# A two-layer attention and gated feed-forward network, forward and backward: transposes by DMA in place of TensorE, weights loaded in pieces, attention products paired, blocks of the feed-forward swapped

## The chip, the cores and the metric

One core of one Trainium2 chip. The time is device microseconds of one execution, the median of several runs. Times inside an execution come from one profiled execution, counted from the start of its span. The engines are TensorE (PE, with weight loads as PEld), VectorE (DVE), ScalarE (ACT), GpSimd (POOL) and SyncE (SP). Every DMA of this kernel is issued from SP's queue, in order: a DMA that has to wait holds up every DMA behind it.

## The reference

The network applies block A, block B, block A, block B to x of shape 2048 x 512, each with a layer normalisation before and a residual around it. The weights of both A blocks are the same, and those of both B blocks. The result is the output and the gradients of x and of all weights, by reverse differentiation from `grad_out`.

```python
def _A_ref(x, wqkv, wo):                      # linear attention, 32 heads of 16
    q, k, v = split_heads(x @ wqkv)
    phi = lambda t: jnp.where(t > 0, t + 1, jnp.exp(t)) + 1e-6
    pq, pk = phi(q), phi(k)
    kv = jnp.einsum("bhsd,bhse->bhde", pk, v)
    z = jnp.einsum("bhsd->bhd", pk)
    num = jnp.einsum("bhqd,bhde->bhqe", pq, kv)
    den = jnp.einsum("bhqd,bhd->bhq", pq, z)[..., None] + 1e-6
    return merge_heads(num / den) @ wo
def _B_ref(x, w_gate, w_up, w_down):          # F = 1376
    h = _sigmoid(x @ w_gate) * (x @ w_up)
    return h @ w_down
x = x + _A_ref(_layernorm(x), A_wqkv, A_wo)   # layer 0
x = x + _B_ref(_layernorm(x), B_w_gate, B_w_up, B_w_down)   # layer 1
x = x + _A_ref(_layernorm(x), A_wqkv, A_wo)   # layer 2
x = x + _B_ref(_layernorm(x), B_w_gate, B_w_up, B_w_down)   # layer 3
```

## The kernel before

The 2048 rows are 16 tiles (`NST`) of 128 rows; two tiles are a pair, four are a block (`NBLK` = 4, 512 rows). D = 512 is four chunks of 128, F = 1376 is eleven chunks (`NFC`), the last of 96.

The order of stages is: `kq_fwd` for layer 0 (keys and queries), `ab_fwd` for layers 0 and 1 together, `kq_fwd` for layer 2, `ab_fwd` for layers 2 and 3, then backward: `BBwd(3).run`, `ABwd(2).first` and `.second`, `BBwd(1).run`, `ABwd(0).first` and `.second`, with the products for the weights' gradients (`p2_gen`) filled in between and at the end.

The order on TensorE, ScalarE, VectorE and GpSimd is the order in which the code issues (`manual_schedule` over these four, `EM`). SP isn't among them. Its order is chosen by the planner of the framework from modelled times, when a DMA's operands are ready there; `issue_after(ins)` only makes a DMA follow another one. On the chip SP then works through that order and waits where something isn't ready yet.

**`ab_fwd`** (line 1050 and on; in the change and below, layer 1 or 3 names its feed-forward half `l`). It goes through the pairs `i` of tiles, `st = 2 * i`. In one pass it does six units of the feed-forward for pair `i`, the second product of the feed-forward (`down_mm`) for the pair before, and the attention for the pair after.

- `gu(st, 2, *CUNITS[u])`: gate and up products of unit `u`: two chunks of F, unit 5 a single one. On TensorE a unit of two is 16 matmuls of 256 columns into the banks `g` and `u` (line 1070). ACT writes the sigmoid into the tile `ssd_t` (line 1086, three buffers) and one minus it into `oms` (1087), DVE the product into `hhT` (1088), POOL the second half of `ssd_t` (1089), and SP stores `ssd_t` (1092). The next use of an `ssd_t` buffer waits for that store.
- `trans`: VectorE transposes `hhT` in blocks into `tr_stg` (1039, two buffers) and SP stores it (1042).
- `ln.apply`, `ln.stage_T`: the normalised rows `hstage`, turned on TensorE (line 568, eight transposes of 128 x 128) into bank `t`, copied by ACT into `hT`, which the next pair's `gu` reads.
- `pair_prod` (POOL), `pair_front1` and `pair_front2` (DVE; the latter ends with `pqnstage`, line 968, stored to DRAM by SP at line 971 for the backward pass) make the normalised queries of pair `i + 2`. `pair_front3` turns them: eight transposes on TensorE (line 982) and an ACT copy (983) into `pqnT2`. `attn_y` of each tile (four matmuls, line 995) then reads them in the next round, right behind the first unit for the first tile and behind the second unit for the second tile; DVE adds the result to x (1003) and takes the statistics of the next normalisation.
- In layer 3, `turn_weights` sends one job at a time of the list from `wT_dmas_b` (line 455 and on), at places between the units: turned loads of `w_down` into `wdT` and their stores, then loads of `wuT` and `wgT`, which `kq_fwd` of layer 2 has turned already, from DRAM. These are the weights of the backward pass.

**`BBwd.run`** (from line 1431) is the backward pass of a feed-forward. For each block of 512 rows and each chunk `u` of F, `D` multiplies `wdT` by the turned gradient `gT` (four matmuls of 512 columns, line 1385), two steps ahead (`LOOK`); ACT copies (1391), DVE and POOL multiply with the stored `ssd` (1392, 1393); `H` multiplies with `wuT` and `wgT` (eight matmuls, line 1417). At the end of a block the normalisation's gradient follows, spread over the next block's steps. `gT` of the next block is made in two halves by `make_gT`: eight transposes on TensorE each (line 1356) and an ACT copy (1357), at steps 5 and 6. In layer 3 (`first`) the gradient is the input `grad_out`, loaded by `load_g` (1337); block 0's is made within the last round of `ab_fwd`, and in block 2 the steps are 7 and 8, with one `D` put behind its `H` (`behind`). In layer 1 the gradient is in `k.xs` in float32; `cast_g` casts it on ACT at steps 1 to 4 into `gstage` (1343) and SP stores it to DRAM as `gbf` (1345), which a later stage reads.

## Time and profile before

| | |
|---|---|
| median of 3 runs | 1132.63 us (1131.1 to 1133.29) |
| profiled execution | 1131.85 us, its span 1130.1 us |
| mean granted TensorE clock | 0.997 |
| TensorE idle in the span, all causes | 35.7 us |
| `ab_fwd` of layer 1 | about 70 to 210 us |
| `ab_fwd` of layer 3 | about 275 to 414 us, transfer engines busy 62% |
| `BBwd` of layer 3 | about 407 to 530 us, transfer engines busy 86% from 414 on |
| `BBwd` of layer 1 | about 737 to 856 us, transfer engines busy 76% from 740 on |
| share of DMA queue q1 over the span | 79.0% |

How to read it: a row of a group gives line, engine, operation, tiles, shape and count, then the group's busy time in us, the mean of one instruction in ns, and the idle time just before such instructions with what ended it. Matmuls are pipelined, so the mean of one is longer than the distance from one to the next. In a timeline a row is start and duration in us, and in brackets the idle time before it and what it waited for. A row of SP with a large duration holds up SP's queue for that long.

### The profile page before, as it was taken

What the parts mean: (1) busy time and instruction counts of PE and PEld (TensorE: products, weight loads), DVE (VectorE), ACT (ScalarE), POOL (GpSimd) and SP (SyncE); (2) the same over time, 40 slices, a digit from 0 to 9 for tenths busy, and PEclk for the clock granted to TensorE, in tenths of its full rate; (3) what the DMA queues carried; (4) which work ended last, traced back from release to release, by engine and by line L of the source; (5) the groups of instructions that cost most, each with busy time, mean ns of one, the idle gap of its engine ahead of it and who ended that gap; (6) DMA issues with size and microseconds to landing.
All of it is one profiled execution on the core that took longest, in us unless ns stands there. A gap on an engine that the chain in (4) does not pass through costs nothing. (4 is left out here: it accounts for less than half of the span.)

```text
span 1130.1 us, 20199 instructions
## 1 busy us (share of the span) xinstructions
PE 1094.4 (97%) x7453; PEld 673.3 (60%) x7556; DVE 718.7 (64%) x1263; ACT 501.9 (44%) x924; POOL 468.1 (41%) x627
## 2 busy tenths in 40 slices
PE   7999999999999899999999999999999999999998
PEld 4467767546776654444665556544446756555577
DVE  7887887888678567776993640057778955642221
ACT  4676656557656533444552441145545523420001
POOL 3738776433766445776110440047772101420000
PEclk9999999999999999999999999999999999999999
DMA  7955657695666768978789967887768999958997
GB/s 218 319 169 160 199 177 222 198 263 177 173 217 187 235 201 265 303 232 278 214 235 265 280 192 253 296 283 225 224 214 223 268 276 253 258 194 272 274 253 166
DMA packets 342612, 263.02 MB, mean 233 GB/s; under 512 B 105648, under 2 KB 321136, under 8 KB 342512
## 3 DMA queue, kind: packets, MB, share of 16 engines
q1 hardware_dynamic: 342512, 261.72, 79.0%
q8 instruction: 59, 0.97, 0.4%
q14 instruction: 41, 0.34, 0.1%
HBM read 122.62 MB, written 119.47 MB: 214 GB/s over the span
## 5 line engine op out<-in xcount | busy, mean ns | idle before, releaser
L1694 PE MATMUL p_ps<-p_set,p_a 128*128 128x384 bf16 (+2 forms) x1792 | 264.6, 304 | 3.3 <-DMA p_set<-sv_hdd 1.5
L1694 PEld LDWEIGHTS <-p_a 128*128 128x128 bf16 x1792 | 168.7, 96 | 87.2 <-issue 3.4
L1393 POOL TENSOR_TENSOR dd<-dhb,ssd 128x512 bf16<-128x512 bf16 x84 | 96.7, 1156 | 106.1 <-ACT dhb L1391 103.9
L1392 DVE TENSOR_TENSOR dd<-dhh_ps,ssd 128x512 bf16<-128x512 f32 x85 | 57.2, 679 | 123.1 <-ACT dhb L1391 121.3
L1417 PE MATMUL dh_ps<-wuT,dd 128*128 128x512 bf16 (+1 forms) x340 | 129.0, 379 | 0.7
L1089 POOL TENSOR_TENSOR ssd_t<-hhT,oms 128x512 bf16<-128x512 bf16 (+1 forms) x92 | 99.7, 1092 | 71.8 <-DVE hhT L1088 50.4
L1417 PE MATMUL dh_ps<-wgT,dd 128*128 128x512 bf16 (+1 forms) x325 | 123.3, 380 | 0.0
L1417 PEld LDWEIGHTS <-dd 128*128 128x128 bf16 x680 | 66.3, 98 | 79.7
L1070 PE MATMUL g_ps<-hT,wg 128*128 128x256 bf16 (+1 forms) x792 | 93.6, 262 | 6.5 <-ACT oms L1087 5.4
L1709 DVE TENSOR_TENSOR dw_stg<-p_ps,dw_stg 128x384 bf16<-128x384 f32 (+2 forms) x76 | 32.0, 438 | 106.4 <-PE p_ps L1694 99.1
L1070 PE MATMUL u_ps<-hT,wu 128*128 128x256 bf16 (+1 forms) x792 | 93.5, 262 | 3.0 <-DVE hhT L1088 3.0
L1391 ACT CAST dhb<-dhh_ps 128x512 bf16<-128x512 f32 x84 | 48.7, 588 | 99.5 <-PE dhh_ps L1385 86.6
L1088 DVE TENSOR_TENSOR hhT<-u_ps,ssd_t 128x512 bf16<-128x512 f32 (+1 forms) x92 | 57.5, 629 | 51.5 <-ACT ssd_t L1086 49.2
L1086 ACT ACTIVATE ssd_t<-g_ps 128x512 bf16<-128x512 f32 (+1 forms) x92 | 51.7, 562 | 86.6 <-PE g_ps L1070 44.4
L1039 DVE STREAM_TRANSPOSE tr_stg<-dd 128x768 f32<-128x768 f32 (+1 forms) x62 | 86.6, 1437 | 1.1
L1070 PEld LDWEIGHTS <-wg 128*128 128x128 bf16 x792 | 70.1, 98 | 27.2 <-issue 8.0
L1385 PE MATMUL dhh_ps<-gT,wdT 128*128 128x512 bf16 x301 | 77.2, 379 | 1.6 <-DVE dd L1392 0.7
L1105 PE MATMUL y_ps<-wd,hhT 128*128 128x512 bf16 (+1 forms) x337 | 77.7, 380 | 0.8
L1070 PEld LDWEIGHTS <-wu 128*128 128x128 bf16 x792 | 70.9, 98 | 12.0 <-issue 4.6
L1711 ACT CAST dw_stg<-p_ps 128x384 bf16<-128x384 f32 (+2 forms) x76 | 28.0, 385 | 88.6 <-PE p_ps L1694 83.8
L1385 PEld LDWEIGHTS <-wdT 128*128 128x128 bf16 x352 | 33.8, 97 | 41.7 <-issue 3.8
L516 POOL TENSOR_TENSOR rstd_all<-rstd_all,neghalf 128x1 f32<-128x1 f32 x64 | 37.9, 592 | 47.7 <-DVE rstd_all L515 43.1
(256 smaller groups left out, 1919.3 us busy)
## 6 DMA issues: line engine op xcount, KB each, us to landing
sv_hdd<-tr_stg SPq DMA_DIRECT2D x72, 384.0 KB, 4.6
p_set<-sv_hdd SPq DMA_DIRECT2D x18, 1536.0 KB, 7.4
sv_ssd<-ssd_t SPq DMA_DIRECT2D x74, 256.0 KB, 2.6
ssd<-sv_ssd SPq DMA_DIRECT2D x23, 768.0 KB, 5.2
h_ld<-sv_h SPq DMA_DIRECT2D x30, 256.0 KB, 4.1
sv_hdl<-tr_stg SPq DMA_DIRECT2D x24, 256.0 KB, 4.8
p_a<-sv_h SPq DMA_DIRECT2D x12, 512.0 KB, 6.5
p_set<-sv_hdl SPq DMA_DIRECT2D x24, 256.0 KB, 4.9
```

The costliest lines, as they stand in the source:

```text
L1039: nc.vector.transpose(t[:, :, 0:n * P].bitcast(F32).rearrange("p q (a j) -> p q a j", a=2 * n), src.rearrange("p c x -> p (c x)").bitcast( ...
L1070: nc.tensor.matmul(ps[:, ci * n:(ci + 1) * n], lhsT=w_sb[:, kc, (c0 + ci) * P:(c0 + ci + 1) * P], rhs=hT[:, kc, (st % 2) * P:(st % 2) * P ...
L1086: nc.scalar.activation(ssd[:, :, 0, :], gv, ACT.Sigmoid)
L1088: nc.vector.tensor_tensor(hh, uv, ssd[:, :, 0, :], ALU.mult)
L1089: nc.gpsimd.tensor_tensor(ssd[:, :, 1, :], hh, oms, ALU.mult)
L1105: nc.tensor.matmul(y_ps[:], lhsT=h[0:r, fc, off:off + P], rhs=k.wd[0:r, fc, :], start=(fc == 0), stop=(fc == NFC - 1))
L1385: nc.tensor.matmul(ps[:], lhsT=k.wdT[:, jc, u * P:(u + 1) * P], rhs=self.gT[B][:, jc, :], start=(jc == 0), stop=(jc == NDC - 1))
L1391: nc.scalar.copy(dhb[:], ps[:])
L1392: nc.vector.tensor_tensor(self.dd[ng][:, 0, c, :], ps[:], self.ssd[ng][:, c, 0, :], ALU.mult)
L1393: nc.gpsimd.tensor_tensor(self.dd[ng][:, 1, c, :], dhb[:], self.ssd[ng][:, c, 1, :], ALU.mult)
L1417: nc.tensor.matmul(self.acc[j][:], lhsT=dd[0:r, a, c, j * P:(j + 1) * P], rhs=w[0:r, u, :], start=(u == 0 and a == 0), stop=(u == NFC - 1 ...
L1694: nc.tensor.matmul(ps[:, 0:w], lhsT=lhs[:, s, ic * P:(ic + 1) * P], rhs=rhs, start=(s == 0), stop=(s == NST - 1))
```

## The change

- `wT_dmas_b`: `wuT` and `wgT` are loaded in five pieces of two chunks each (256 KB) in place of a piece of six chunks and one of four. In layer 3 `turn_weights` is called at up to four places of a round in place of one or two.
- `pair_front3`: the turned queries are loaded from DRAM, where `pair_front2` has stored them, by a transposing DMA on SP, in place of eight transposes and a copy. The early pair of each pass is still turned on TensorE.
- `attn_y` of both tiles of a pair stand together behind the first unit.
- The units 4 and 5 of the feed-forward are swapped around `stage_T`, except in the last round; `pair_front3` stands ahead of both.
- In layer 1's pass `ssd_t` has five buffers, in a pool of its own, and `tr_stg` four.
- `BBwd`: `turn_g` loads `gT` by two transposing DMAs, in layer 3 from the input for all blocks, in layer 1 from the stored `gbf` at step 6 for the blocks 1 to 3. Block 0 of layer 1 is still turned on TensorE. The special order in block 2 of layer 3 goes, but for the late load of its `gstage`.

```diff
@@ wT_dmas_b
-        for c, e in ((0, 6), (6, NFC - 1)):
+        for c in range(0, NFC - 1, 2):
+            e = c + 2
             jobs.append(lambda nm=nm, t=t, c=c, e=e: nc.sync.dma_start(out=t[:, c:e, :],
                                                                        in_=view(k.wT[nm + "T"][c * P:e * P, :])))
@@ attn_fronts
-    def pair_front3(i):
+    def pair_front3(i, dma=True):
...
+        if dma:
+            turned = pool.tile([P, NDC, 2 * P], BF16, name="pqnT2", bufs=2)[:]
+            nc.sync.dma_start_transpose(out=turned, in_=sva["pqn"][batch_rows(i, 2), :])
+            pqnT = turned.rearrange("p c (n t) -> p n c t", n=2)
+        else:
...
@@ ab_fwd
+        more = ctx.enter_context(tc.tile_pool(name=f"bf_more{l}", bufs=5, reuse_waits="tile")) if l == 1 else None
...
-                ssd_f = work.tile([P, 2 * BT], BF16, name="ssd_t", bufs=3)
+                ssd_f = (more or work).tile([P, 2 * BT], BF16, name="ssd_t", bufs=5 if more else 3)
...
-            block_transposes(k, work, sv, 0, B, g, hhT[B][:, c0:c0 + nch, :], bufs=2)
+            block_transposes(k, work, sv, 0, B, g, hhT[B][:, c0:c0 + nch, :], bufs=4 if l == 1 else 2)
...
-        A.pair_front3(2)
+        A.pair_front3(2, False)
...
             gu(st, 2, *CUNITS[0])
+            if l == 3 and i > 1:
+                turn_weights()
             A.attn_y(st + 2, "t")
+            A.attn_y(st + 3, "t")
             A.pair_front1(i + 2)
             after(st - 3)
             gu(st, 2, *CUNITS[1])
-            A.attn_y(st + 3, "t")
             A.pair_front2(i + 2)
...
             if l == 3 or i % 2 == 0:
                 turn_weights()
-                if l == 3 and i > 3:
-                    turn_weights()
...
             gu(st, 2, *CUNITS[3])
+            if l == 3:
+                turn_weights()
             down_mm(st - 1, "t")
...
-                if bwd is not None:
-                    bwd.make_gT(0, 0)
-            gu(st, 2, *CUNITS[4])
+            A.pair_front3(i + 2)
+            gu(st, 2, *CUNITS[5 if not last else 4])
             ln.stage_T([st + 2, st + 3], bank="t")
-            A.pair_front3(i + 2)
             after(st - 2)
-            if last and bwd is not None:
-                bwd.make_gT(0, 1)
-            gu(st, 2, *CUNITS[5])
+            gu(st, 2, *CUNITS[4 if not last else 5])
+            if l == 3:
+                turn_weights()
@@ BBwd.load_g
         if self.first:
+            self.turn_g(B)
             nc.sync.dma_start(out=t[:], in_=dram_batch(k.g_in, B))
+    def turn_g(self, B):
+        if B not in self.gT:
+            self.gT[B] = self.alloc(False, "work", [P, NDC, BT], "gT", 2)
+        for half in range(2):
+            self.k.nc.sync.dma_start_transpose(out=self.gT[B][:, :, half * 2 * P:(half + 1) * 2 * P],
+                                               in_=self.sv["gbf"][batch_rows(2 * B + half, 2), :])
@@ BBwd.run
-                    behind = self.first and B == 2 and u == 9
...
-                    if not close and not behind:
+                    if not close:
                         self.D(n + self.LOOK)
                     self.H(B, u)
-                    if behind:
-                        self.D(n + self.LOOK)
...
-                        if u in ((7, 8) if late else (5, 6)):
-                            self.make_gT(B + 1, 0 if u in (5, 7) else 1)
+                        if u == 6 and not self.first:
+                            self.turn_g(B + 1)
```

More of the change, by code (lines that the diff above doesn't have):

```diff
@@ L977, in pair_front3 @@
         pqn = F_[2 * i]["pqn"]
-        pqnT = pool.tile([P, 2, NDC, P], BF16, name="pqnT2", bufs=2)
-        ps = ps_tile(k, "ln", [P, 2, NDC, P], BF16, "ln_tp")
-        for j in range(2):
-            for c in range(NDC):
-                nc.tensor.transpose(ps[:, j, c, :], pqn[:, j, c * P:(c + 1) * P], k.ident[:])
-        nc.scalar.copy(pqnT[:], ps[:])
+        if dma:
[3 more added lines that the diff above has]
+        else:
+            pqnT = pool.tile([P, 2, NDC, P], BF16, name="pqnT2", bufs=2)[:]
+            ps = ps_tile(k, "ln", [P, 2, NDC, P], BF16, "ln_tp")
+            for j in range(2):
+                for c in range(NDC):
+                    nc.tensor.transpose(ps[:, j, c, :], pqn[:, j, c * P:(c + 1) * P], k.ident[:])
+            nc.scalar.copy(pqnT, ps[:])
         for j in range(2):
```

## The prediction

> **What bounds the kernel now.** I read the busy shares first, then the idle time of TensorE by what ended it, then the timeline where it idles longest, then the landing times of the transfers that would take over work. The page's first part, and one row of the stretches of 20 us:

> ```profile
> span 1130.1 us, 20199 instructions
> PE 1094.4 (97%) x7453; PEld 673.3 (60%) x7556; DVE 718.7 (64%) x1263; ACT 501.9 (44%) x924; POOL 468.1 (41%) x627
> ...
> 372.00:392.00 20.00, 16.02 (x110) 11.01 (x109) 12.40 (x17) 8.65 (x15) 7.05 (x11) 0.91 0.72 228
> ```

> TensorE is busy 97% of the span: what is taken off TensorE counts almost in full, and what makes TensorE wait costs in full. The 20 us from 372 to 392, in the second feed-forward pass (the `ab_fwd` of layer 3), are the worst of the passes: 4 us idle, and a mean clock of 0.91. The timeline there (weight loads of PE left out; start, duration, engine, line):

> ```profile
> 367.94 0.61 PE L982 MATMUL ln_tp<-ident,pqnstage 128*128 128x128 bf16 x8
> 368.35 1.12 SPq L465 DMA_DIRECT2D wgT<-wgT_d  x2
> 368.39 0.60 PE L1070 MATMUL g_ps<-hT,wg 128*128 128x256 bf16 x4
> ...
> 377.39 0.60 ACT L1086 ACTIVATE ssd_t<-g_ps 128x512 bf16<-128x512 f32 x1 [6.00 <-DMA sv_ssd<-ssd_t]
> ...
> 378.53 1.87 PE L1070 MATMUL g_ps<-hT,wg 128*128 128x256 bf16 x8 [3.70 <-ACT oms L1087]
> ```

> Two loads of `wgT` (768 and 512 KB) go out together at 368.35; the small `sv_ssd` stores behind them land late, so ACT waits 6.00 us for one of three `ssd_t` buffers, and TensorE 3.70 us for ACT. The eight matmuls then take 1.87 us in place of 1.04: the clock records show half speed for 3.41 us from 379.2. The first and third line also give the price of a turn on TensorE: eight transposes start at 367.94, the next matmul at 368.39, so 0.45 us. Which sets there are, by shape:

> ```profile
> L1356 PE MATMUL gT_ps<-ident,gstage 128*128 128x128 bf16 x112 | 8.4, 220 | 0.1
> L982 PE MATMUL ln_tp<-ident,pqnstage 128*128 128x128 bf16 x96 | 7.4, 220 | 0.2 <-DVE pqnstage L968 0.2
> L1356 PE MATMUL gT_ps<-ident,pre_gstage 128*128 128x128 bf16 x16 | 1.2, 219 | 0.0
> ```

> And the transfers that matter (KB each where plain, then median us from issue to landing):

> ```profile
> sv_pqn<-pqnstage SPq DMA_DIRECT2D x16, 256.0 KB, 2.1
> h_ld<-sv_h SPq DMA_DIRECT2D x30, 256.0 KB, 4.1
> sv_gbf<-gstage SPq DMA_DIRECT2D x4, 512.0 KB, 5.0
> pkT_ld<-sv_pk SPq DMA_TRANSPOSE x14, 4.3
> wt_gu<-in_B_w_up_dram SPq DMA_TRANSPOSE x5, 4.0
> ```

> **The change part by part.** The sum is made against the profiled execution, 1131.85 us (span 1130.1); the median of the runs, 1132.63, is 0.8 above it.

> *Turns leave TensorE.* Of the 12 sets of line 982, two (the early pair of each pass) stay and 10 go. Of the 16 sets of line 1356 (14 plus 2 of `pre_gstage`), layer 3 loses all 8 and layer 1 keeps those of its first block, so 14 go. 24 sets x 0.45 = 10.8 us. The `B` stretches run TensorE 115.0 of 116 us, so nothing but TensorE is the bound there; I take all 10.8 (floor 0.97 of it, 10.4). 24 ACT copies of about 1.02 us go too; ACT is busy 44%, so alone they give nothing.

> *Weights in 256 KB pieces (layer 3).* 9 jobs become 15, 6 more issues of about 0.5 us on SP, which mostly waits; I cost them at nothing, SP's waits for `ssd_t` (91.7 us in total) being the cover. All are sent by the fourth pair, up to four in a pair. The stall goes: 3.7 idle plus 1.7 for 3.41 us at half clock; so should the 1.0 idle at 339, also on ACT, after the 768 KB `wuT` load at 332.6. Together 6.4. The other end is 0, if other stores hold the three buffers as long.

> *More buffers in layer 1* (5 `ssd_t`, 4 `tr_stg`). ACT waited there 13.3 us in 11 pieces for stores, but TensorE idled just 4.0 us in that pass on named engines, 2.8 of it on DVE's `hhT`. I take 1.0 (the one idle of 1.12 at 155.9); ends 0 and 4.0.

> *Two attention products together, blocks swapped.* TensorE does the same matmuls. The second product (0.86 us) with its DVE add (0.68), statistics (0.87) and three small POOL steps moves ahead of the second block; SP and DVE get the same work in another order, and DVE has hardly a gap from the first add to the end of `pqnstage` (304.3 to 311.1 in one pair). The single-chunk block (0.87 us) now stands before the turn of `hT`, the double one (1.73) behind it, which covers the ACT copy of 1.01 better. Idle on `hT` was 0.5 us in both passes; the turn now comes 0.87 earlier behind a normalisation that had 2.1 us to spare. Ends -0.5 and +1.0; I take 0, nearest to that idle row.

> *gT in layer 3.* Eight turned loads straight from the input. Their plain loads went out at 417.9, 429.6 and 487.3 for blocks whose first product stood at 438.07, 467.72 and 499.08: 12 us or more, against 1.3 on SP for the first of two and 4.0 to land. I cost them at 0. The transfer engines have a share of 0.86 there, so `ssd` loads may land later; two steps of lookahead on TensorE (5.2 us) cover that, and DVE's and POOL's waits for `ssd` (6.4 us) reach TensorE nowhere now. The one product of block 2 that stood behind its neighbour goes back in front of it, at nothing: the late `gT` that it gave way to is gone.

> *gT in layer 1, three blocks.* Here a wait is added. The source is the store of `gstage`, issued at 753.50, 783.19 and 812.82 and landing 6.8, 5.0 and 5.1 us later. The first product of the next block stands 10.1 us behind the store's issue, and 9.2 once the two sets of turns between are gone. The two loads must wait for the landing: 1.26 on SP for the first (rows of `wt_gu`), 4.0 to land for the second, so 10.3 (12.1 for the first block). TensorE stands still 2.9 + 1.1 + 1.2 = 5.2, and the `ssd` load of 768 KB that SP issues at the same time (788.20) adds some 0.3 to each: I take +6.0. Queued behind the waiting load on SP are that `ssd` load and the `hdd` stores; the lookahead covers them. Ends: 0 (a 2.9 us landing, the shortest of the four, leaves 8.2) and +12 (6.8 for each, plus one half clock of 1.7 and 2 more on SP).

> *Normalised queries by load.* From the end of `pqnstage` on DVE to the product that needs it there were 5.7 us (the first pair that is moved) and 8.1 to 8.6 in layer 1, 6.3 and 6.6 to 6.8 in layer 3; less 0.45 now. The chain needs 2.1 (store) + 0.1 + 4.0 = 6.2 if SP issues the load as the store lands. Layer 1: the first pair 1.0 late, the rest in time: +1.0. Layer 3: four pairs late by 0.1 at most, together 0.2; the first pair meets the `wdT` turn on SP (2.42 us at 296.78), so it has 5.9 for 8.6 and is 2.7 late, an estimate from that row: +2.9. Ends: 0, and if the load stands behind the next `ssd` store on SP, issued 3.4 after `pqnstage`, 1.8 more in each late pair: +4 and +13.

> Sum: -10.8 - 6.4 - 1.0 + 0 + 6.0 + 1.0 + 2.9 = **-8.3**, so 1123.6 in a profiled execution and **1124** as the median.

> [...] In the trace a turned 256 KB load lands in 4.0 to 4.3, like the plain `h_ld` with 4.1, but holds SP 1.25 us and more where a plain issue holds it 0.36, and moves in packets of 256 bytes that take the 16 engines 1.66 us by the packet records, a plain 256 KB 0.75. [...]

> **The rivals.**
> 1. *Everything lands in time.* For it: pairs with 8 us to spare, and a store that landed in 2.9. Against: the three 10.1 us windows. -10.8 - 6.4 - 1.0 gives 1114.4.
> 2. *The query loads stand behind the `ssd` stores on SP.* For it: SP runs in order and its longest waits are for exactly these stores. Against: the load is ready 1.2 us before that store is. 1.8 in each of five pairs in layer 3 and two in layer 1 is 12.6; less the 2.9 that layer 3 has already, 1134: no change, or a little slower.
> 3. *Slower: layer 3's three `ssd_t` buffers.* A turned load that waits on SP holds back the `ssd` stores, and TensorE sees again what it saw at 374.8, now in pair after pair: 5.4 us each with the clock. Two such stalls eat the forecast gain (8.3 / 5.4 = 1.5); three in the five pairs give 1124 + 16.2 = 1140. For it: ACT waited ten times, 24.7 us, for these stores in layer 3. Against: no transfer as large as 1280 KB is left in one go.
> 4. *The pieces don't mend the stall*: the 6.4 stays, 1130.

> **How the numbers follow.** Forecast 0.46 (1118 to 1129), rival 1 0.16, rival 2 0.19, rival 3 0.15, rival 4 0.04. A measurement of this kernel can't tell less than 0.2% (2.3 us) from no change. Faster: forecast, rival 1 and little of 2 and 4, 0.66; same: most of 2, 0.13; slower 0.21. The range 1114 to 1139 cuts part of rivals 1 and 3.

> **What would show it.** Lines of transposes x16 in place of x112 and x16; clock 1.00 in layer 3's pass and no wait of 3 us on `oms`; idle of TensorE before the first product of a block in layer 1 on a DMA into `gT`, 1 to 3 us each; before the attention products on a DMA into `pqnT2`, largest in layer 3's first pair. Wrong, if those two sum to much other than 9.9, or if waits on `oms` appear in several pairs. [...]

## The result and the profile after

The changed kernel takes 1164.37 us (median of 4 runs, 1163.22 to 1165.46) where the kernel before takes 1132.47 beside it: a ratio of 1.0283, 95% interval 1.0265 to 1.0301. It is 2.8% slower, 31.9 us; the forecast was 8 us faster.

The page's first lines, of the kernel after:

```profile
span 1162.0 us, 19817 instructions
PE 1093.9 (94%) x7263; PEld 665.7 (57%) x7364; DVE 724.7 (62%) x1263; ACT 480.4 (41%) x900; POOL 461.3 (40%) x627
```

190 fewer matmul records on TensorE (24 sets of eight are 192) and 24 fewer instructions on ACT: the turns did leave. But TensorE is busy as long as before (1094.4; part of it at half speed, as shown below), and the span is 31.9 longer. Line numbers in a view are those of the kernel that it shows, so the store of `ssd_t`, line 1092 before, is L1099 here. The idle time of TensorE by what ended it (us in total, times, longest), of the kernel after:

```profile
PE y_ps L1001 <- DMA pqnT<-sv_pqn: 20.1, 7, 4.6
PE dhh_ps L1401 <- DMA gT<-sv_gbf: 18.2, 3, 7.4
PE dh_ps L1433 <- DVE junk L1256: 3.0, 2, 2.8
...
PE u_ps L1077 <- DVE hhT L1095: 1.0, 2, 0.6
```

The first two lines are the two round trips of the change, write to DRAM and load back turned: 38.3 us of idle where the forecast had 9.9. `junk` (L1256) is the first step of the normalisation's gradient on DVE. Waits on `oms` are gone, as forecast. Now the busy time of each engine in six stretches, with the granted clock as the third figure from the end; the cuts are the first product of `ab_fwd` in layer 1, the start of `kq_fwd` of layer 2, its end, the first `D` and last `H` of `BBwd(3)`, and those of `BBwd(1)`:

```profile
70.50:221.20 150.70, 138.55 (x1105) 99.66 (x1122) 118.71 (x189) 81.25 (x142) 94.94 (x143) 0.95 0.65 179
221.20:274.50 53.30, 51.39 (x302) 25.86 (x307) 45.19 (x87) 30.36 (x51) 16.45 (x18) 1.00 0.97 261
274.50:418.60 144.10, 132.04 (x1098) 97.39 (x1112) 105.66 (x161) 78.42 (x144) 80.38 (x101) 0.98 0.67 199
418.60:542.20 123.60, 119.01 (x545) 53.96 (x554) 86.53 (x106) 45.59 (x90) 83.48 (x84) 1.00 0.92 284
542.20:749.10 206.90, 204.98 (x1377) 124.93 (x1393) 99.60 (x214) 80.19 (x172) 35.70 (x68) 1.00 0.84 241
749.10:889.00 139.90, 119.63 (x522) 52.85 (x531) 82.62 (x100) 51.05 (x99) 81.70 (x80) 0.94 0.71 212
```

With the same cuts the kernel before has 140.7, 53.3, 143.7, 122.3, 207.3 and 118.1; its last row is

```profile
737.20:855.30 118.10, 116.67 (x568) 54.33 (x579) 82.09 (x101) 56.63 (x105) 81.67 (x80) 1.00 0.75 238
```

So layer 1's pass lost 10.0, layer 3's pass 0.4 (the pieces gained there what the queries lost), layer 3's backward stretch 1.3 and layer 1's 21.8. In the three stretches with the round trips the clock is below 1 (0.95, 0.98 and 0.94): the records show half speed in eight places that the kernel before does not have, each beginning within or right behind an idle of 2.7 us or more, five of them 3.41 us long and three of them 6.8.

How the round trips went, from SP's queue (start, us the instruction held SP, line). Of the kernel after, one pair in layer 3, then the last block of layer 1's backward pass:

```profile
342.90 0.38 SPq L972 DMA_DIRECT2D sv_pqn<-pqnstage  x1
344.39 0.53 SPq L1048 DMA_DIRECT2D sv_hdd<-tr_stg  x1
346.26 0.36 SPq L1099 DMA_DIRECT2D sv_ssd<-ssd_t  x1
346.67 0.52 SPq L466 DMA_DIRECT2D wgT<-wgT_d  x1
347.45 0.36 SPq L1099 DMA_DIRECT2D sv_ssd<-ssd_t  x1
347.86 0.50 SPq L466 DMA_DIRECT2D wgT<-wgT_d  x1
348.45 0.52 SPq L556 DMA_DIRECT2D sv_h<-hstage  x1
349.07 1.42 SPq L981 DMA_TRANSPOSE pqnT<-sv_pqn  x1
```

```profile
844.41 1.25 SPq L1352 DMA_TRANSPOSE gT<-sv_gbf  x1
845.76 0.52 SPq L1382 DMA_DIRECT2D ssd<-sv_ssd  x1
846.38 1.21 SPq L1048 DMA_DIRECT2D sv_hdd<-tr_stg  x2
847.64 4.22 SPq L1352 DMA_TRANSPOSE gT<-sv_gbf  x1
```

The store of `pqnstage` is issued at 342.90 and lands 4.4 later (in the other nine pairs 2.1 to 2.4); the turned load goes out at 349.07, 6.2 behind it, because SP's order has an `hdd` store, two `ssd` stores, two weight pieces and `sv_h` ahead of it, and the stores wait for their own engines. In the ten pairs the distance is 3.5, 7.1, 3.8, 7.1, 3.8 (layer 1) and 5.8, 6.3, 6.2, 6.2, 3.8 (layer 3). For `gT` the order of the last two blocks puts a load of `ssd` and two `hdd` stores between the two halves, and the second half of the last block then holds SP for 4.22; it goes out 8.2 behind the store of `gbf` at 839.41.

### The profile page after: what moved, and what is told of

It is laid out like the page before. It is cut to its first block, busy times and chain, and to the rows that moved or that the text cites. A ratio compares the mean times of both kernels' runs of the same rounds, so it can differ in the third digit from the quotient of the medians.

```text
span 1162.0 us, 19817 instructions
## 1 busy us (share of the span) xinstructions
PE 1093.9 (94%) x7263; PEld 665.7 (57%) x7364; DVE 724.7 (62%) x1263; ACT 480.4 (41%) x900; POOL 461.3 (40%) x627
## 5 line engine op out<-in xcount | busy, mean ns | idle before, releaser
L1096 POOL TENSOR_TENSOR ssd_t<-hhT,oms 128x512 bf16<-128x512 bf16 (+2 forms) x92 | 99.7, 1092 | 71.2 <-DVE hhT L1095 32.7
L1433 PE MATMUL dh_ps<-wgT,dd 128*128 128x512 bf16 (+1 forms) x329 | 126.8, 385 | 0.1
L1401 PE MATMUL dhh_ps<-gT,wdT 128*128 128x512 bf16 x300 | 78.4, 384 | 21.0 <-DMA gT<-sv_gbf 18.2
L1093 ACT ACTIVATE ssd_t<-g_ps 128x512 bf16<-128x512 f32 (+2 forms) x92 | 51.4, 559 | 110.1 <-PE g_ps L1077 103.2
L1095 DVE TENSOR_TENSOR hhT<-u_ps,ssd_t 128x512 bf16<-128x512 f32 (+2 forms) x92 | 57.5, 630 | 28.8 <-ACT ssd_t L1093 18.4
L1094 ACT ACTIVATE oms<-g_ps 128x512 bf16<-128x512 f32 (+2 forms) x96 | 53.6, 559 | 7.8 <-POOL ssd_t L1096 7.1
## 6 DMA issues: line engine op xcount, KB each, us to landing
sv_ssd<-ssd_t SPq DMA_DIRECT2D x74, 256.0 KB, 2.8
h_ld<-sv_h SPq DMA_DIRECT2D x30, 256.0 KB, 4.3
sv_hdl<-tr_stg SPq DMA_DIRECT2D x24, 256.0 KB, 5.3
p_a<-sv_h SPq DMA_DIRECT2D x12, 512.0 KB, 6.3
p_set<-sv_hdl SPq DMA_DIRECT2D x24, 256.0 KB, 4.9
```

What stands on the lines that cost most here:

```text
L1093: nc.scalar.activation(ssd[:, :, 0, :], gv, ACT.Sigmoid)
L1094: nc.scalar.activation(oms, gv, ACT.Sigmoid, scale=-1.0)
L1095: nc.vector.tensor_tensor(hh, uv, ssd[:, :, 0, :], ALU.mult)
L1096: nc.gpsimd.tensor_tensor(ssd[:, :, 1, :], hh, oms, ALU.mult)
L1401: nc.tensor.matmul(ps[:], lhsT=k.wdT[:, jc, u * P:(u + 1) * P], rhs=self.gT[B][:, jc, :], start=(jc == 0), stop=(jc == NDC - 1))
L1433: nc.tensor.matmul(self.acc[j][:], lhsT=dd[0:r, a, c, j * P:(j + 1) * P], rhs=w[0:r, u, :], start=(u == 0 and a == 0), stop=(u == NFC - 1 ...
```

## The experiments

All ratios are to the kernel before, measured beside the run, with 95% intervals. Stretches are those of the table above.

**One round trip undone at a time.** `gT` of layer 1 back on TensorE, then the queries, then both:

```diff
-                        if u == 6 and not self.first:
-                            self.turn_g(B + 1)
+                        if u in (5, 6) and not self.first:
+                            self.make_gT(B + 1, u - 5)
```

> The changed kernel, with gT of layer 1's blocks 1 to 3 turned on TensorE again at steps 5 and 6. Theory (the turned loads land late, and each stop of TensorE also brings half clock): the stretch of layer 1's backward feed-forward, 139.9 us in the changed kernel and 118.1 before, goes back to about 118, so about 1164.4 - 21.8 = 1142.6. Rival A (only the idle time counts, the half clock is hidden elsewhere): 18.2 less idle, 2.7 more for six sets of turns, 1148.9. Rival B (the stretch is longer for another reason, transfers in each other's way): little changes, above 1155.

Measured: 1139.45 us, 1.0053 (1.0036 to 1.0070). Layer 1's backward stretch is 118.5 us in place of 139.9.

```diff
-            A.pair_front3(i + 2)
+            A.pair_front3(i + 2, False)
```

> The changed kernel, with all normalised queries turned on TensorE again. Theory: 20.1 us of waits for the turned queries go, and six half-clock windows of 3.41 us with them (1.7 each, 10.2), 4.5 comes back for ten sets of turns: about 1138.6. Rival A (the half clock costs nothing on top): 1148.8. Rival B (the small store buffers of layer 3 are what holds the pass): waits on oms of ACT come in place of the waits for queries in layer 3, and little is won there.

Measured: 1143.22 us, 1.0099 (1.0073 to 1.0125). Layer 1's pass 137.4, layer 3's pass with the stage ahead of it 190.6 (after: 197.4).

> Both undone at once; the weights in pieces, the buffers, the paired products, the swapped blocks and layer 3's gT by DMA stay. Theory (the two late loads carry the whole loss): 1164.4 - 21.8 - 25.8 = 1116.8, faster than the kernel before by some 1.4%. Rival C (the rest of the change costs too): between 1125 and 1135.

Measured: 1122.38 us, 0.9905 (0.9877 to 0.9932). Without the two round trips the change gains. The idle list of TensorE of the first two kernels, one line each, and the top of the third's:

```profile
PE y_ps L1001 <- DMA pqnT<-sv_pqn: 17.4, 7, 4.3
```

```profile
PE dhh_ps L1401 <- DMA gT<-sv_gbf: 17.0, 3, 6.6
```

```profile
PE dh_ps L1433 <- DVE junk L1256: 3.7, 2, 3.4
```

By the differences of the ratios (times 1132.5): queries 16.8 us, `gT` in layer 1 22.0, and 4.0 more when both are there. The time of the first kernel came out 3 us below what was expected of it, those of the second and third 5 and 6 above: what the third still loses is in layer 3's backward stretch, taken up below.

**Pieces of the weights alone**, on the kernel before:

```diff
-        for c, e in ((0, 6), (6, NFC - 1)):
+        for c in range(0, NFC - 1, 2):
+            e = c + 2
...
+            if l == 3 and i > 1:
+                turn_weights()
...
```

> The kernel before with only the weights in 256 KB pieces, at the changed kernel's places. Theory: the idle of 3.7 at 374.8 with its half clock of 1.7 and the 1.0 at 339 go: 1132.5 - 6.4 = 1126.1. Rival D (the pieces only move the stores' delay elsewhere): 1131 to 1134, with new waits on oms.

Measured: 1125.62 us, 0.9936 (0.9918 to 0.9955). The stretch that lost 4 us before, cut as before:

```profile
372.00:392.00 20.00, 19.77 (x151) 14.24 (x150) 13.32 (x20) 11.48 (x21) 9.76 (x14) 1.00 0.62 199
```

TensorE idles 0.2 of 20 us and the clock is full. This term of the sum held: 7.2 us for 6.4.

**The loads one block, or some units, earlier.** First `gT` of layer 1: `cast_g` and its store run a block ahead, and the turned loads go out at step 0 of the block before their use.

```diff
+                        if u == 0 and not self.first:
+                            self.turn_g(B + 1)
+                            self.load_g(B + 2)
...
-                            self.cast_g(B + 1, u - 1)
+                            self.cast_g(B + 2, u - 1)
...
```

> The changed kernel, with the cast and store of layer 1's gradients one block earlier (blocks 0 and 1 ahead of the loop, then block B+2 at steps 1 to 4 of block B) and the turned loads of block B+1 at step 0 of block B: the same turned loads, with a whole block of time. Theory (what costs is only that they start too late): 1139.5 of the run with turns on TensorE, less 2.7 for six sets of turns, 1136.8. Rival E (turned loads cost by their traffic and their time on SP, wherever they stand): no better than 1139.5, idle of TensorE elsewhere in the stretch.

Measured: 1139.80 us, 1.0055 (1.0036 to 1.0073); no wait on `gT` left, and the stretch is 115.5 us, 2.9 less than with the turns on TensorE (118.5). So the saving of the turns (six sets, 2.7) is there once the load is out early. In the total these 2.9 don't show beside 1.0053; its runs spread from 1136.8 to 1145.0.

Then the queries: `pair_front1`, `2` and `3` together right behind the first unit, ahead of the products.

```diff
+            A.pair_front1(i + 2)
+            A.pair_front2(i + 2)
+            A.pair_front3(i + 2)
             A.attn_y(st + 2, "t")
             A.attn_y(st + 3, "t")
-            A.pair_front1(i + 2)
...
```

> The changed kernel, with the last two steps of the normalised queries on VectorE and the turned load issued right behind the first unit, ahead of the two attention products of the same round, so that the load stands directly behind its store on SP and 5 us or so earlier. Theory: the waits for queries, 20.1, fall under 3 and most of the six half-clock windows go: 1143.2 of the run with queries on TensorE, less 4.5 for ten sets of turns, 1138.7. Rival E: waits on ACT's oms or VectorE's hhT in their place, above 1143.

> Both of these. Theory: 1122.4 of the run with both on TensorE, less 7.2 for sixteen sets of turns, 1115.2. Rival E: above 1122.

Measured: 1150.88 us, 1.0140 (1.0111 to 1.0170), and with `gT` early too 1122.49, 0.9894 (0.9863 to 0.9925). The idle list of the first, top two lines:

```profile
PE dhh_ps L1401 <- DMA gT<-sv_gbf: 20.3, 3, 8.5
PE u_ps L1077 <- DVE hhT L1095: 7.6, 8, 2.3
```

No wait on `pqnT`, but the steps of the queries on DVE now stand ahead of `hhT`, which TensorE needs: 7.6 us come back under another name. Both were expected lower. With both early the passes are 139.1 and 190.6, some 1.6 longer each than with the queries on TensorE (137.4, 189.1): the ten sets of turns that leave there (4.5 us) are not gained.

**The half clock by itself.** Before the first product of a block in layer 1 stand 14, 28 and 30 matmuls of 512 columns whose results nothing reads; TensorE works where it would wait.

```diff
+        if not self.first and u == 0 and B:
+            junk_ps = ps_tile(k, "ln", [P, BT], F32, "junk_ps")
+            for i in range(WAIT[B]):
+                nc.tensor.matmul(junk_ps[:], lhsT=k.wdT[:, 0, 0:P], rhs=k.wdT[:, 1, 0:BT], start=True, stop=True)
...
```

> The changed kernel, with 14, 28 and 30 matmuls of 512 columns (3.0, 6.0 and 6.5 us at full clock) on TensorE ahead of the first product of layer 1's blocks 1, 2 and 3, where it idles 3.9, 6.9 and 7.4: the loads are as late as they were, only the idle time is filled; their results are not used. Theory (the half clock after an idle stop costs on its own): no half clock in this stretch, 17 us of it before at 0.5, so 1164.4 - 8.5 = 1156. Rival A (it costs nothing on top): 1164.

Measured: 1158.12 us, 1.0209 (1.0168 to 1.0250). The stretch has full clock and is 134.6 us for 139.9. So the 17.1 us at half clock there cost at least 5.3 us (2.8 us of waits on `gT` are left), and the waits the rest. By the ratios it is 8.4 us, but the runs of this kernel spread from 1154.5 to 1163.5.

**All turns back, then the best of both.** With the turns of layer 3's `gT` on TensorE as well (`load_g` without `turn_g`, `make_gT` at its old places), and then with layer 1's `gT` by early loads as above:

> The changed kernel with all three kinds of turns on TensorE (queries, gT of layer 1, gT of layer 3); the pieces, the buffers, the paired products and the swapped blocks stay. Theory: in layer 3's backward feed-forward the turned loads cost more than they save, because they push the load of h behind other work on SP (idle 3.7 on DVE's junk, and half clock behind it). With them gone that stretch goes back from 124.5 to the 122.3 of the kernel before, so 1122.4 - 2.2 = about 1120. Rival (the prediction's own zero for these loads): eight sets of transposes come back on TensorE at 0.45 each and nothing is mended, 1122.4 + 3.6 = 1126.

Measured: 1121.17 us, 0.9885 (0.9867 to 0.9904). Layer 3's backward stretch, with the turned loads (queries and layer 1 on TensorE) and without any:

```profile
396.10:520.60 124.50, 120.87 (x555) 54.34 (x553) 86.39 (x106) 45.60 (x90) 83.59 (x84) 0.99 0.91 282
```

```profile
397.80:520.10 122.30, 121.91 (x602) 56.57 (x602) 86.33 (x105) 50.97 (x95) 82.72 (x84) 1.00 0.84 273
```

With the loads TensorE is busy 1.0 us less (47 matmuls fewer, but 3.4 us at half clock), and the stretch takes 2.2 longer; the transfer engines are busier (0.91 for 0.84). The place is the end of block 1, where DVE needs `h_ld` to begin the normalisation's gradient. DVE and SP in the kernel after:

```profile
486.96 0.75 DVE L1256 SCALAR_TENSOR_TENSOR junk<-dh_ps,rstd_all,h_ld 128x512 bf16<-128x512 f32 x1 [3.38 <-DMA h_ld<-sv_h]
```

```profile
478.30 0.34 SPq L1382 DMA_DIRECT2D ssd<-sv_ssd  x1
478.92 1.49 SPq L1048 DMA_DIRECT2D sv_hdl<-tr_stg  x2
480.51 1.02 SPq L1386 DMA_DIRECT2D h_ld<-sv_h  x1
```

In the kernel before:

```profile
465.85 1.53 SPq L1370 DMA_DIRECT2D h_ld<-sv_h  x1
468.31 0.34 SPq L1366 DMA_DIRECT2D ssd<-sv_ssd  x1
468.93 1.50 SPq L1042 DMA_DIRECT2D sv_hdl<-tr_stg  x2
```

That `h_ld` stood ahead of the load of `ssd` and of the `hdl` stores; now it stands behind them. A DMA that the change does not touch had been given another place. It took no longer to land (6.3 us from its issue, before 7.0), so the busier transfer engines are not what made it late.

> As the one with all turns on TensorE, but gT of the last three blocks of layer 1 turned by loads that go out one block earlier. Theory: such loads are waited for by nobody, and the stretch falls from 118.5 to the 115.5 that it had with early loads, 2.9 less: about 1117. Rival: the early loads take the transfer engines from the ssd loads and the stores, and the time stays at 1120.

Measured: 1118.46 us, 0.9870 (0.9852 to 0.9889), the fastest kernel of this study, 1.3% below the kernel before. Its backward stretch of layer 1 (725.9 to 842.4):

```profile
725.90:842.40 116.50, 114.94 (x533) 51.70 (x531) 82.28 (x100) 48.97 (x95) 81.76 (x80) 1.00 0.84 246
```

Full clock and 1.6 us of idle, with four turned loads in it and two ahead of it. It is 1.6 shorter than with the turns on TensorE (118.1); the two totals can't be told apart.

**Order or turning?** First the query load is issued in the code right behind `pair_front2`, nothing else moved:

```diff
             A.pair_front2(i + 2)
+            A.pair_front3(i + 2)
             trs(nt)
...
-            A.pair_front3(i + 2)
```

> The changed kernel with the turned load of the queries issued in the code right behind the store that it reads (two units earlier), with nothing else moved. Theory (the place in SP's order is what makes the queries late): the distance from store to load on SP falls from 3.5 to 7.1 us to about 2 to 4, the idle on pqnT from 20.1 us to about 8, and the half clock behind these idles goes in most pairs: 1150 to 1154. Rival (the turned load itself takes that long, or holds SP so that the ssd stores are late in its place): idle moves to ACT's oms, and the time stays within 3 us of 1164.

Measured: 1151.56 us, 1.0151 (1.0119 to 1.0183), 15 us better than the change. The same pair of layer 3 as above on SP, and the idle that is left:

```profile
329.16 0.56 SPq L972 DMA_DIRECT2D sv_pqn<-pqnstage  x1
330.64 0.52 SPq L1048 DMA_DIRECT2D sv_hdd<-tr_stg  x1
332.50 0.36 SPq L1099 DMA_DIRECT2D sv_ssd<-ssd_t  x1
332.96 1.30 SPq L981 DMA_TRANSPOSE pqnT<-sv_pqn  x1
```

```profile
PE y_ps L1001 <- DMA pqnT<-sv_pqn: 7.1, 5, 2.5
```

The load now stands behind one `ssd` store in place of two and the weights: 2.7 to 3.8 behind its store in all ten pairs. Then the loads of the queries and of layer 1's `gT` as plain ones of the same bytes, at the places of the change. The rows arrive unturned, so the products work on other values, with the same instructions:

> The changed kernel with the loads of the queries and of gT in layer 1 (blocks 1 to 3) as plain loads of the same bytes from the same place, so that the rows arrive unturned: the attention of both layers' moved pairs and the backward pass behind gT compute from unturned operands, with the same instructions. Theory (the round trip through DRAM in SP's order is the cost): only the issue on SP (1.25 to 4.2 us turned, about 0.4 plain) and a part of the landing get shorter; the first product of the three blocks in layer 1 gains some 2 us each from the second load's issue, the queries about 0.5 in each of 11 pairs: about 1152. Rival (the turning is the cost): the idles on pqnT and gT all but go, about 1125.

Measured: 1155.64 us, 1.0190 (1.0162 to 1.0219). The loads from issue to landing (median us), of the kernel after and of this one, and this one's idle:

```profile
pqnT<-sv_pqn SPq DMA_TRANSPOSE x10, 4.3
gT<-in_grad_out_dram SPq DMA_TRANSPOSE x6, 5.8
gT<-sv_gbf SPq DMA_TRANSPOSE x6, 4.1
```

```profile
pqnT<-sv_pqn SPq DMA_DIRECT2D x10, 256.0 KB, 4.2
...
gT<-sv_gbf SPq DMA_DIRECT2D x6, 256.0 KB, 3.0
```

```profile
PE y_ps L1001 <- DMA pqnT<-sv_pqn: 19.3, 7, 4.0
PE dh_ps L1438 <- DVE junk L1256: 7.3, 4, 3.1
PE dhh_ps L1406 <- DVE dd L1413: 3.7, 3, 1.6
PE dhh_ps L1406 <- DMA gT<-sv_gbf: 2.8, 1, 2.8
```

For the queries turning costs nothing: 19.3 us of idle for 20.1, at the same distances on SP (7.1, 3.8, 6.2 and so on). For `gT` it costs part: layer 1's backward stretch is 131.6 for 139.9, since the two plain loads go out 0.41 apart instead of 3.2 with other work between. Of the 21.8 us lost there, 8.3 hang on the turned kind and what it does to SP's order, 13.5 remain with a plain load of the same place.

Little of these 13.5 is a wait for `gT`: only the first block has one (2.8 us). In the other two VectorE waits for the `tr_stg` buffers that the `hdd` stores behind the loads free. These stores go out 0.5 to 1.9 us after their data are ready and land 6.8 to 8.1 after that; in the kernel before, at the same place in block 1, it is 0.03 and 3.9 to 4.4. In layer 1's stretch of this run:

```profile
DVE tr_stg L1045 <- DMA sv_hdd<-tr_stg: 8.8, 3, 4.3
```

The kernel after has 8.3 us there in two waits, the kernel before none. TensorE then waits for VectorE, under `dd` and `junk`, and 10.2 us of half clock come with it. How the 13.5 divide among these is not shown.

**Which part gave more than forecast.** The change without the three kinds of turns gains 13.0 us, the pieces 7.2 of it. On the pieces, first the buffers of layer 1 alone, then the paired products and swapped blocks without the buffers:

```diff
-                ssd_f = work.tile([P, 2 * BT], BF16, name="ssd_t", bufs=3)
+                ssd_f = (more or work).tile([P, 2 * BT], BF16, name="ssd_t", bufs=5 if more else 3)
...
```

> The kernel before with the weights in pieces and, in layer 1's pass, five buffers of ssd_t and four of tr_stg; the attention products, the blocks and all turns stay as before. With all turns on TensorE the whole rest of the change (pieces, buffers, paired products, swapped blocks) gave a ratio of 0.9885, pieces alone 0.9936, and layer 1's pass went from 140.8 to 137.4 us. Theory (the buffers did it, since layer 3's pass, which has the pairing and the swap but no buffers, stayed at 189.4 against 189.3): layer 1's pass 137.4, ratio about 0.989 to 0.990. Rival (the pairing and the swap did it): layer 1's pass 140.8, ratio 0.9936.

> The changed kernel with all turns on TensorE and the buffers of ssd_t and tr_stg as before: pieces, paired products and swapped blocks alone. Theory (the buffers did it): layer 1's pass 140.8, ratio 0.9936. Rival (the pairing and the swap did it): 137.4 and about 0.989. If both are needed, both of these runs stay near 0.9936.

Measured: 1122.46 us, 0.9892 (0.9875 to 0.9909), and 1126.74, 0.9936 (0.9916 to 0.9956). Layer 1's pass in the one and the other:

```profile
69.30:206.90 137.60, 135.94 (x1160) 100.31 (x1161) 115.74 (x189) 85.16 (x148) 98.60 (x143) 1.00 0.63 187
```

```profile
70.00:211.10 141.10, 136.55 (x1160) 100.29 (x1161) 117.64 (x188) 85.60 (x147) 94.95 (x143) 1.00 0.60 183
```

The buffers did it; the pairing and the swap are worth nothing that can be measured.

## Why the prediction was wrong

Term by term, in us against 1132.5; measured values are differences of the ratios above, each uncertain by some 2 to 3:

| term | forecast | measured |
|---|---|---|
| weights in pieces | -6.4 | -7.2 |
| more buffers in layer 1 | -1.0 | -5.0 (-3.2 in the pass itself) |
| paired products, swapped blocks | 0 | 0 |
| `gT` in layer 3, with 8 sets off TensorE | -3.6 | +2.3 |
| `gT` in layer 1, with 6 sets off TensorE | 3.3 | 22.0 |
| queries, with 10 sets off TensorE | -0.6 | 16.8 |
| both of these at once, and what is left over | | 3.2 |
| sum | -8.3 | 32.1 |

*The step that failed most* is the clause "if SP issues the load as the store lands", in the query chain of 6.2 us. Nothing made SP do that: its order is fixed ahead, and the loads got places 3.5 to 7.1 us behind their stores (2.2 to land), behind DMAs that wait for other engines. Moving the place alone gave back 15 us; taking the turning away at the same place gave next to nothing. Rival 2 had this mechanism, and the upper end of the term too, but both priced it at one `ssd` store (1.8 us in seven pairs): 12.6, where idle alone is 20.1 and the half clock comes on top. Its reason against, "the load is ready 1.2 us before that store is", does not count: readiness did not decide, the order did.

*For `gT` in layer 1 the window was right and the chain too short.* The products wanted `gT` 9.6, 9.5 and 8.5 us behind the store's issue (start of the product less the idle before it), as the forecast 9.2. They got it after 13.5, 16.4 and 15.9, where the forecast had 12.1, 10.3 and 10.3. The first half did go out about as the store landed (7.8, 6.1 and 5.0 behind it). The second, put at "1.26 on SP for the first" and 4.0 to land, went out 2.1, 3.2 and 3.2 behind the first, and from there it was another 3.6, 7.2 and 7.6 to the product, 1.50, 3.82 and 4.22 of that on SP. The `ssd` load and the `hdd` stores were named as queued behind the waiting load, with "the lookahead covers them". In the last two blocks they stand between its halves, and the lookahead did not cover the stores: VectorE waited 8.3 us for their buffers, beside TensorE's wait for `gT`; with plain loads, where that wait was all but gone, it was 8.8.

*The half clock was priced too low.* The `gT` term had one half clock in its upper end and none in the +6.0 itself. The trace shows it behind idles of 2.76, 3.19, 4.01, 4.59 and 2.72 in the passes and 3.91, 6.91 and 7.38 in layer 1's `BBwd`. In that stretch it cost at least 5.3. (The one half clock of the kernel before, put at 379.2, runs from 378.25 on the scale of the timeline, just ahead of the end of the idle at 378.53.) The stretch adds up: 18.2 idle, 5.3 of clock, 2.7 less for the turns is 20.8 of the 21.8.

*"I cost them at 0"* for the turned loads from the input: their own arrival was indeed hidden (no wait on them), but they changed the place of `h_ld`, and the 3.6 us of turns came back as a loss of 2.2 in the stretch. The cover named, two steps of lookahead, is a cover for `ssd` and not for `h_ld`, which has a use once a block and none to spare.

*What held*: the price of a turn, 0.45, where it could be seen (six sets of layer 1, 2.7: early loads shorten the stretch by 2.9 in one comparison and 1.6 in the other; what the sets of the queries and of layer 3 should have saved no run gained); the pieces; the zero for pairing and swap; no waits on `oms`, so rival 3 (the three buffers of layer 3) did not come, and rival 4 neither. The buffers were mis-sized: 1.0 was one idle of 1.12 on `hhT`, while all of that row, 2.8 us in six pieces, falls to 0.9, and TensorE's idle in the pass from 4.8 to 1.7 (window less busy time). The range, 1114 to 1139, ended 25 us short of the result. Even all upper ends together (-10.4 + 0 + 0 + 1.0 + 0 + 12 + 4 + 13 = 19.6) would have given only 1152: without the turns that they save, the queries cost 21.3 where their upper ends make 17, `gT` in layer 1 24.7 where its upper end is 12.

## What to carry to other kernels

The round trips of the queries through DRAM were priced by where the load stood in the queue (20.1 us of idle, 7.1 after the place alone was moved), not by the kind of load (19.3 with plain ones at the same place): list every DMA between the store and the load, and ask what each of them waits for, and what stands behind the load while it waits. If the order is chosen by a planner, assume that every added DMA may move its neighbours too, and look for loads with no slack. Turned loads that went out a block early shortened layer 1's backward stretch by 1.6 to 2.9 us; the same loads issued where the value was just ready cost 18.2 us of idle there and at least 5.3 for the half clock with it.

## What the runs showed of the hardware

Turned and plain loads of 256 KB of the queries from the same place landed alike, 4.3 and 4.2 us. Those of `gT` in layer 1 didn't, 4.1 and 3.0. On SP they differ: a turned query load took 1.29 to 2.40 us, a plain one 0.49 (at 121.32 in the run with plain loads); a turned load of `gT` in layer 1 took 1.25 to 4.22, most for the second half where other DMAs stood between, and two plain ones together 1.70 and 0.87 (at 774.68 and 806.77 in that run); the turned loads from the input took 1.26 to 3.92. What SP waits for in that time no run shows.
